# A 4-byte tile of ones is allocated behind the buffer of exponentials in a fused attention and MLP kernel

## The chip, the cores and the metric

One core of a Trainium2 chip runs the whole kernel. The metric is the device time of one execution in microseconds (us); the figure for a kernel is the median of its runs.

## The reference

Sliding-window attention over 8 batches, 8 heads, 576 positions and 64 features, then an MLP over the 4608 tokens of 512 features.

```python
scores = scale * np.matmul(q, k.transpose(0, 1, 3, 2))
mask = (rel >= 0) & (rel < window)                 # window = 128
scores = np.where(mask, scores + bias[None], -1000000000.0)
scores = scores - np.max(scores, axis=-1, keepdims=True)
attn = np.exp(scores)
attn = attn / (np.sum(attn, axis=-1, keepdims=True) + 1e-09)
attn_out = np.matmul(attn, v)
x = np.ascontiguousarray(attn_out.transpose(0, 2, 1, 3)).reshape(B * S, H * D)
h = x @ w_in                                       # 512 -> 2048
g = 0.5 * h * (1.0 + erf(h * inv_sqrt2))
return g @ w_out                                   # 2048 -> 512
```

## The kernel before

The tokens are cut into nine tiles of 512 (`t` = 0 to 8), and the attention into eight batches of four pairs of heads, 32 units. Batch 0 is computed in float32; from batch 1 on every operand is split into a high and a low float16 part, and a product is three matmuls. The order of all instructions is written out by hand in the table `ORDER`, so a change of addresses doesn't move any of them.

The attention of one batch after the first goes like this. `load_qk` brings q and k by DMA into two rooms, `ld_0` and `ld_1`, and `load_v` brings v into `v32`. `split_qk` and `split_v` write the two parts of each into `qbuf`, `kbuf` and `vbuf` (ScalarE the high part, VectorE at L335 the low one). `scores` multiplies them (L667), `biased` adds scale and bias into the tile `s` (L693), and `softmax` finds the maxima (L781) and the exponentials (L785) and scales them (L795). The high parts go into the buffer of exponentials `e_main` at L797 (L792 in batch 1) and `low_weights` puts the low parts there at L805 (L335 in batch 1). There is one `e_main`, [128 partitions, 9 groups, 2 parts, 256] in float16, for all units.

At L809 a DMA transpose, issued on SP's queue, then brings `e_main` into the tile `et`, in two pieces for each unit, one of five groups and one of four:

```python
yield nc.sync.dma_start_transpose(
    st.et[:, r.start * 4 : r.stop * 4, :], e[:, r].rearrange("p g h k -> p (g h k)")
)
```

Units with an even number write the buffer `et0`, those with an odd number `et1`. There are 28 such units, so 56 transposes. `weigh` multiplies `et` by `vbuf` on TensorE (L854), and `leave` writes the result into the tokens' tile `x`, which has two buffers used in turn.

The MLP multiplies `x` by `w_in` (L904 in the first three tiles, L1133 later, where sums of the tokens, `xs`, and of the weights, `t` from the DRAM tile `stored`, take part), applies GELU into `g`, and multiplies by `w_out` (L947, L950, and L1283 in the last two tiles). In the last two tiles `qbuf`, `kbuf`, `vbuf` and `e_main` are free and hold sums of weights that DMAs bring there (L1048, L1052). The sums are written to DRAM at L1041 from the rooms `ld_0` and `ld_1`, in turn.

The tile of ones, `one`, is a single float32 on one partition. It is set once (L288) and is the stationary operand of the 16 matmuls at L300, which spread a maximum over the partitions (`over_partitions` with `early`).

All of these tiles lie in one pool. A tile takes a multiple of 32 bytes of each partition, and tiles stand in memory in the order in which they are first asked for in the program's text.

Of the kernel before, what the change touches and what calls it, by code (L numbers as in the profile page):

```python
# [11 lines left out]
F32 = mybir.dt.float32  # L12
# [194 lines left out]
def attention_gelu_mlp(  # L207
# [10 lines left out]
    nc = tc.nc  # L218
    pool = ctx.enter_context(tc.tile_pool(name="sb", bufs=1))
# [64 lines left out]
    QP = 32  # L284
    square = pool.tile([QP, QP], F32, name="square")
    nc.vector.memset(square, 0.0)
    one = pool.tile([1, 1], F32, name="one")
    nc.vector.memset(one, 1.0)  # L288

    spreads = []  # L290

# [414 lines left out]
        yield nc.gpsimd.memset(e[:, ODD, :, 0:QB], 0.0)  # L706

    e_main = pool.tile([P, NG, 2, 256], F16, name="e_main")


    e_first = [e.rearrange(p).bitcast(F32)[:, 0 : NG * 256].rearrange("p (g k) -> p g k", g=NG)
# [805 lines left out]
```

## Time and profile before

| | |
|---|---|
| median of 3 runs | 874.44 us (871.98 to 876.07) |
| the profiled execution | 873.86 us, its span 872.1 us |
| granted TensorE clock | 0.998 |
| busy share of the span | PE 97%, DVE 81%, ACT 70%, POOL 39% |
| instructions | 19752 |

PE is TensorE's matmuls, PEld its weight loads, DVE VectorE, ACT ScalarE, POOL GpSimd and SP the engine that issues the DMAs. A matmul's busy time is modelled: matmuls overlap in the array, so a busy PE isn't always a PE at its peak. Idle time of an engine is shown beside what ended it. DMA transfers run on 16 DMA engines; a view of DMAs gives their busy share in tenths and the GB/s that they moved in 40 equal slices of the stretch that was asked for.

### The profile page before, as it was taken

What the parts mean: (1) busy time and instruction counts of PE and PEld (TensorE: products, weight loads), DVE (VectorE), ACT (ScalarE), POOL (GpSimd) and SP (SyncE); (2) the same over time, 40 slices, a digit from 0 to 9 for tenths busy, and PEclk for the clock granted to TensorE, in tenths of its full rate; (3) what the DMA queues carried; (4) which work ended last, traced back from release to release, by engine and by line L of the source; (5) the groups of instructions that cost most, each with busy time, mean ns of one, the idle gap of its engine ahead of it and who ended that gap; (6) DMA issues with size and microseconds to landing.
All of it is one profiled execution on the core that took longest, in us unless ns stands there. A gap on an engine that the chain in (4) does not pass through costs nothing.

```text
span 872.1 us, 19752 instructions
## 1 busy us (share of the span) xinstructions
PE 842.9 (97%) x7876; PEld 549.3 (63%) x7876; DVE 706.8 (81%) x1275; ACT 612.0 (70%) x1234; POOL 342.9 (39%) x553
## 2 busy tenths in 40 slices
PE   7899999999999999999999998998999999999997
PEld 4644444544544455884578556864587467888886
DVE  5998999899889966889797988799778656784772
ACT  6978879888769967775677776764776547753671
POOL 5731000033024774479635965576435670000000
PEclk9999999999999999999999999999999999999999
DMA  9855666642563557555846396447752493412301
GB/s 306 286 161 201 230 188 116 152 161 57 102 144 98 137 133 207 194 128 150 188 143 187 104 212 177 127 86 188 187 188 56 110 200 152 188 50 85 110 1 50
DMA packets 180940, 129.47 MB, mean 148 GB/s; under 512 B 134384, under 2 KB 157040, under 8 KB 177136
## 3 DMA queue, kind: packets, MB, share of 16 engines
q1 hardware_dynamic: 180848, 128.21, 53.3%
q8 instruction: 62, 1.02, 0.5%
q14 instruction: 30, 0.25, 0.1%
HBM read 75.89 MB, written 17.83 MB: 107 GB/s over the span
## 4 chain that ended last, share of the span: by engine, by line
PE 55%; DVE 19%; DMA 10%; ACT 8%; issue 4%; POOL 3%; SPq 0%; DVEq 0%; ACTq 0%; POOLq 0%
PE u L1133 12%; PE v L1133 9%; PE h L904 9%; DMA et<-e_main 7%; PE o L950 6%; PE o L947 5%; PE u_out L1283 4%; DMA k<-kp 3%; DVE g L335 3%; PE sc L667 3%; DVE s L693 2%; DVE e_main L805 2%; DVE nmax L781 2%; PE av L854 1%; PE z_out L1283 1%
## 5 line engine op out<-in xcount | busy, mean ns | idle before, releaser
L950 PEld LDWEIGHTS <-g 128*128 128x128 f16 x1152 | 111.0, 98 | 131.2
L950 PE MATMUL o<-wo,g 128*128 128x512 f16 x864 | 192.2, 379 | 0.0
L785 ACT ACTIVATE s<-s,nmax 128x192 f32<-128x192 f32 x252 | 112.0, 446 | 46.8 <-DVE nmax L781 46.5
L904 PE MATMUL h<-x,wi 128*128 128x512 f16 x576 | 128.6, 379 | 1.9 <-DVE wi L335 1.6
L795 POOL TENSOR_SCALAR s<-s,z 128x192 f32<-128x192 f32 x180 | 100.9, 576 | 25.0 <-DVE z L789 11.5
L1133 PEld LDWEIGHTS <-t 128*128 128x128 f16 x1008 | 98.4, 98 | 11.8
L904 PEld LDWEIGHTS <-wi 128*128 128x128 f16 x576 | 54.8, 98 | 67.8 <-DVE wi L335 1.9
L1133 PEld LDWEIGHTS <-wi 128*128 128x128 f16 x864 | 83.9, 98 | 13.4 <-issue 1.3
L699 POOL MEMSET s<- 64x128 f32 (+1 forms) x112 | 19.3, 173 | 157.2 <-DVE s L693 143.6
L693 DVE SCALAR_TENSOR_TENSOR s<-sc,cs,bias_h 128x384 f32<-128x384 f32 x112 | 65.6, 606 | 2.0 <-PE sc L667 1.1
L950 PE MATMUL o<-wo_moved,g 128*128 128x512 f16 x288 | 66.0, 379 | 0.0
L781 DVE TENSOR_REDUCE nmax<-s 128x5 f32<-128x960 f32 (+1 forms) x56 | 58.4, 1047 | 3.4 <-POOL s L699 2.5
L1133 PE MATMUL u<-xs,t 128*128 128x256 f16 x504 | 59.9, 273 | 0.0
L947 PE MATMUL o<-zo,g 128*128 128x512 f32 x128 | 57.6, 599 | 0.0
L854 PE MATMUL av<-et,vbuf 128*64 128x128 f16 (+2 forms) x1392 | 43.7, 220 | 13.7 <-DMA et<-e_main 13.7
L805 DVE TENSOR_TENSOR e_main<-s,e_main 128x960 f16<-128x960 f32 (+1 forms) x40 | 46.5, 1168 | 11.4 <-ACT e_main L797 11.3
L667 PE MATMUL sc<-kbuf,qbuf 64*64 64x192 f16 (+3 forms) x1656 | 49.3, 251 | 6.3 <-DMA kbuf<-kp 4.6
L854 PEld LDWEIGHTS <-vbuf 128*64 128x64 f16 x1392 | 40.3, 111 | 23.4 <-issue 17.9
L1184 POOL TENSOR_SCALAR g<-rooms,sg 128x512 f16<-128x512 f32 x48 | 39.5, 830 | 24.7 <-ACT rooms L1178 21.5
L785 ACT ACTIVATION_READ_ACCUMULATOR s<-s,nmax 128x1 f32 x252 | 47.7, 189 | 0.0
L335 DVE SCALAR_TENSOR_TENSOR g<-rooms,sg,g 128x512 f16<-128x512 f32 x48 | 40.6, 864 | 8.0 <-POOL g L1184 7.9
L797 ACT CAST e_main<-s 128x960 f16<-128x960 f32 (+1 forms) x40 | 36.1, 907 | 14.5 <-POOL s L795 10.4
(256 smaller groups left out, 1698.6 us busy)
## 6 DMA issues: line engine op xcount, KB each, us to landing
t<-stored SPq DMA_DIRECT2D x21, 1024.0 KB, 5.2
v<-vp SPq DMA_DIRECT2D x32, 320.0 KB, 5.4
out<-ob SPq DMA_DIRECT2D x34, 256.0 KB, 2.8
raw<-w_in SPq DMA_DIRECT2D x8, 1024.0 KB, 10.7
raw<-w_out SPq DMA_DIRECT2D x8, 1024.0 KB, 6.1
q<-qp SPq DMA_DIRECT2D x7, 1152.0 KB, 5.8
k<-kp SPq DMA_DIRECT2D x7, 1152.0 KB, 7.1
stored<-sums SPq DMA_DIRECT2D x8, 512.0 KB, 2.7
```

The source lines that it names most:

```text
L335: return nc.vector.scalar_tensor_tensor(out=dst, in0=src, scalar=scale, in1=high, op0=ALU.mult, op1=ALU.subtract)
L667: done = nc.tensor.matmul(ps[bank][o, n, gap:W], a, m[:, gap:W], start=(i == 0 and (n == 0 or b > 0)), stop=(i == len(terms) - 1 and b > 0 ...
L693: yield nc.vector.scalar_tensor_tensor(out=s[:, bank[0] : bank[0] + k, :], in0=ps[bank][:, 0:k, 0:W], scalar=cs, in1=bias.broadcast_to([P, ...
L781: yield nc.vector.tensor_reduce(out=nmax[:, r], in_=s[:, r], axis=AX.X, op=ALU.max, negate=True)
L785: yield nc.scalar.activation(s[:, i, :], s[:, i, :], AF.Exp, bias=nmax[:, i : i + 1], accum_out=z[:, i : i + 1])
L795: yield nc.gpsimd.tensor_scalar(to, s[:, i], z[:, i : i + 1], 1.0, op0=ALU.mult, op1=ALU.mult)
L805: yield engine.tensor_tensor(out=e[:, r, 1, c], in0=st.s[:, r], in1=e[:, r, 0, c], op=ALU.subtract)
L854: done = nc.tensor.matmul(av[r, (js[0] - blocks[0]) * QB : (js[-1] + 1 - blocks[0]) * QB], v32s[b][:, hp, kb, r] if b < EXACT else vbuf[:, ...
L904: done = nc.tensor.matmul(ph, wi[n][:, a, cc, k * P : (k + 1) * P], x[:, cc, b, :], start=(i == 0), stop=(i == 3 * NCC - 1),)
L947: done = nc.tensor.matmul(o, g[:, r, c], zo[n][:, n % 2, k * DM : (k + 1) * DM], start=(fc == first), stop=(fc == last))
L950: done = nc.tensor.matmul(o, g[:, r, a, c], (wo if t else wo_first)[n][:, b, k, :], start=(fc == first and i == 0), stop=(fc == last and i ...
L1133: done = nc.tensor.matmul(ps[:, k * HT : (k + 1) * HT], w(a, i)[:, k * P : (k + 1) * P], m(b, i), start=first and n == 0, stop=True, skip_ ...
```

## The change

The two lines that allocate `one` and set it to 1 move from behind the tile `square` to behind `e_main`.

```diff
     square = pool.tile([QP, QP], F32, name="square")
     nc.vector.memset(square, 0.0)
-    one = pool.tile([1, 1], F32, name="one")
-    nc.vector.memset(one, 1.0)
...
     e_main = pool.tile([P, NG, 2, 256], F16, name="e_main")
+    one = pool.tile([1, 1], F32, name="one")
+    nc.vector.memset(one, 1.0)
```

On VectorE, at the start of the program, the memset of `one` stands here before (`adders` holds the identity matrices):

```order
L260 MEMSET adders 128x128
L286 MEMSET square 32x32
L288 MEMSET one 1x1
L264 COPY adders<-adders 64x64 x4
L265 COPY adders<-adders 128x64
```

and here in the changed program:

```order
L260 MEMSET adders 128x128
L286 MEMSET square 32x32
L708 MEMSET one 1x1
L264 COPY adders<-adders 64x64 x4
L265 COPY adders<-adders 128x64
```

It has kept its place, and so has every other instruction on every engine and queue, with its waits. What differs is where tiles lie. Byte at which a tile starts in each partition, in the two built programs:

```
tile                        bytes   before    after   after minus before
square                        128     6272     6272     0
one                            32     6400    45056     +38656
pww, sww, ... s2 (8 tiles)     32 each, 6432 to 6656 before    -32
qbuf                         9216     6688     6656     -32   (before 13*512 + 32)
kbuf                         9728    15904    15872     -32   (before 31*512 + 32)
vbuf                        10240    25632    25600     -32   (before 50*512 + 32)
e_main                       9216    35872    35840     -32   (before 70*512 + 32)
x, one of its two buffers    8192    45088    45088     0     (32 past a multiple of 64)
x, the other                 8192   129920   129920     0     (a multiple of 64)
et0                          9216    75552    75552     0     (32 past a multiple of 64)
et1                          9216   112448   112448     0     (a multiple of 64)
ld_0                         9216    84768    84768     0     (32 past a multiple of 64)
ld_1                         9216   175040   175040     0     (a multiple of 64)
g, two of four               8192    60320, 121696      0     (32 past a multiple of 64)
g, the other two             8192   104256, 138112      0     (multiples of 64)
```

All other tiles stay where they were. In the table a multiple of 64 is never one of 256, but for the four large buffers that move, which start at multiples of 512 after the change.

## Rows read from the trace of the kernel before

**Rows 1.** The page, parts 1 and 2: busy time of the engines; busy tenths by slice.
```profile
PE 842.9 (97%) x7876; PEld 549.3 (63%) x7876; DVE 706.8 (81%) x1275; ACT 612.0 (70%) x1234; POOL 342.9 (39%) x553
...
PE   7899999999999999999999998998999999999997
...
PEclk9999999999999999999999999999999999999999
```

**Rows 2.** The list of waits: who waited for whom, us in total, times, longest.
```profile
PE av L854 <- DMA et<-e_main: 13.7, 10, 2.9
...
PEld L854 <- DMA et<-e_main: 5.5, 3, 2.1
...
PE sc L667 <- DMA kbuf<-kp: 4.6, 1, 4.6
```

**Rows 3.** The view of line 854: idle time of its engine (us, times) until
```profile
  DMA et<-e_main: 19.2, 13
```

**Rows 4.** The chain that ended last: shares by line; pieces (start us, us).
```profile
PE u L1133 12%; PE v L1133 9%; PE h L904 9%; DMA et<-e_main 7%; PE o L950 6%; PE o L947 5%; PE u_out L1283 4%; DMA k<-kp 3%; DVE g L335 3%; PE sc L667 3%; DVE s L693 2%; DVE e_main L805 2%; DVE nmax L781 2%; PE av L854 1%; PE z_out L1283 1%
...
149.12 5.41 DMA et<-e_main
...
709.31 6.61 DMA et<-e_main
```

**Rows 5.** The tile e_main: duration in ns (min/median/max), first and last start; landings.
```profile
L809 SPq DMA_TRANSPOSE et<-e_main x56: 1541/3066/5885, 119.2 to 713.0; - x56
L797 ACT CAST e_main<-s x40: 816/906/994, 275.8 to 710.8; 128x960 f16<-128x960 f32 x20, 128x768 f16<-128x768 f32 x20
L805 DVE TENSOR_TENSOR e_main<-s,e_main x40: 943/1147/1701, 278.9 to 711.6; 128x960 f16<-128x960 f32 x20, 128x768 f16<-128x768 f32 x20
...
DMA to landing us min/median/max: 4.2/5.0/9.8
```

**Rows 6.** DMAs of the stretch 206 to 213 us (slices of 0.175 us).
```profile
GB/s 0 0 0 0 0 0 0 0 0 0 10 170 221 218 203 209 217 215 227 214 217 221 214 219 222 215 215 168 119 87 224 214 217 206 209 217 218 224 214 218
DMA packets 4105, 1.04 MB, mean 149 GB/s; under 512 B 4105, under 2 KB 4105, under 8 KB 4105
```

**Rows 7.** DMAs of the stretch 220 to 229.5 us (slices of 0.24 us).
```profile
GB/s 0 0 0 0 0 0 0 0 87 224 213 204 221 217 218 217 218 216 213 212 182 103 205 212 168 27 8 188 292 287 290 291 285 6 0 0 0 0 0 0
DMA packets 4673, 1.19 MB, mean 125 GB/s; under 512 B 4672, under 2 KB 4672, under 8 KB 4672
```

**Rows 8.** DMA issues of the stretch 257 to 261 us (KB each, us to landing).
```profile
stored<-sums SPq DMA_DIRECT2D x1, 512.0 KB, 2.8
```

**Rows 9.** DMAs of the stretch 266 to 271 us (slices of 0.125 us).
```profile
GB/s 12 0 0 0 0 0 0 0 0 0 0 0 0 0 0 0 0 197 328 426 426 426 360 426 426 393 459 328 0 0 0 0 0 0 0 0 0 0 0 0
...
stored<-sums SPq DMA_DIRECT2D x1, 512.0 KB, 2.6
```

**Rows 10.** Views of the tiles x, e_main and g, and of line 1133: duration in ns.
```profile
L904 PE MATMUL h<-x,wi x576: 376/379/390, 35.5 to 298.3; 128*128 128x512 f16 x192
...
L1133 PE MATMUL u<-xs,t x504: 269/273/283, 359.5 to 837.4; 128*128 128x256 f16 x168
...
L1283 PE MATMUL u_out<-e_main,slots x48: 272/273/273, 787.0 to 862.2; 128*128 128x256 f16 x48
...
L1283 PE MATMUL u_out<-wo,g x72: 272/273/283, 737.2 to 846.5; 128*128 128x256 f16 x72
...
L1224 ACT ACTIVATE g<-room_s,sg x24: 708/723/727, 726.0 to 856.6; 128x512 f16<-128x512 f32 x24
L335 DVE SCALAR_TENSOR_TENSOR g<-room_s,sg,g x24: 741/749/754, 726.7 to 857.4; 128x512 f16<-128x512 f32 x24
```

**Rows 11.** The tile one: duration in ns (min/median/max).
```profile
L300 PEld LDWEIGHTS spread<-red,one x16: 180/182/184, 28.4 to 124.3; 1*128 1x128 f32 x16
...
L288 DVE MEMSET one<- x1: 59/59/59, 1.0 to 1.0; 1x1 f32 x1
```

## The prediction, made before the changed kernel ran

> **What bounds the kernel now.** Start with the page's busy times [rows 1]. TensorE is busy 842.9 of 872.1 us, at nine tenths or more in nearly every slice, at the full granted clock. So an edit that leaves its matmuls alone can win only what TensorE idles, 872.1 - 842.9 = 29.2 us, and an edit that delays something off TensorE costs only what comes through to it. Then read the list of waits for the idle time that has an address in it [rows 2]. The largest such item is the wait of the matmuls and weight loads of L854 for the transposed exponentials: 13.7 + 5.5 = 19.2 us, 13 times, which the view of that line confirms [rows 3]. The chain that ended last passes through the same transposes [rows 4]: 7% of it lies in ten pieces between 149 and 716 us, of which the first and the last are shown. The share says where the path runs; it doesn't say how much of it would be saved, for where a transpose lands sooner TensorE takes up the slack after 19.2 us at most.
>
> **What the change removes, adds and moves.** It adds no instruction and takes none away, and on no queue does one pass another. The memset of 59 ns [rows 11] keeps its place on VectorE, and the 16 weight loads of `one`, 180 to 184 ns each, read the same single number from another address. I cost both at zero; there is no cover to lose, because nothing has moved in time. What is left is the 32 bytes by which `qbuf`, `kbuf`, `vbuf` and `e_main` slide down: from 32 past a multiple of 512 to a multiple of 512. So the sum has one kind of term, the price of an address. I take it apart by who uses these buffers.
>
> *TensorE, ScalarE, VectorE.* The trace already holds both kinds of address for them. The 576 matmuls at L904 read the two buffers of `x` in turn, one at a multiple of 64 and one 32 past it, and all take 376 to 390 ns. L1133 reads `xs`, 32 past a multiple of 64, in 273 ns; L1283 reads `e_main`, 32 past, in 273 ns, and `wo` in the same 273. ScalarE writes four buffers `g`, two of each kind, in 708 to 727 ns, and VectorE in 741 to 754 [rows 10]. The spread over both kinds is under 3%, so the term is zero, with ends that I can't tell from zero.
>
> *The first loads and the last.* The four loads each of q and k at the start land in buffers that move, and TensorE waits 4.6 us for one [rows 2]. The end of the gain is some part of that once; I take zero. The six loads of weight sums at the end appear in no wait of TensorE in the list, so their price is hidden by the matmuls of the stretch.
>
> *The 56 transposes.* This is the term that matters. Each reads `e_main` and lands after 4.2 to 9.8 us, median 5.0 [rows 5]. The larger piece moves 128 partitions x 5 groups x 512 numbers x 2 bytes = 655 KB, and its packets are all under 512 bytes [rows 6]. Its steady rate is about 217 GB/s, so 655 KB take 3.02 us of the landing. Is that rate set by an address? For the destination the trace answers: those of the one stretch write `et0`, 32 past a multiple of 64 [rows 6], those of the other stretch `et1`, at a multiple [rows 7], and both run at 203 to 227 GB/s, mostly 213 to 221. For the source no transpose of the trace has another address, since there is one `e_main`. The nearest row is another DMA that reads the same memory: the store of sums at L1041 lands after 2.8 us from `ld_0`, 32 past a multiple of 64 [rows 8], and after 2.6 us from `ld_1`, a multiple [rows 9]. The 0.2 us between them lies within what a slice of these rows can tell, and neither start is a multiple of 256. I take **zero for each transpose**, and keep both ends for the range. The end of the gain: packets of 4 KB leave at about 426 GB/s [rows 9], by which 655 KB would take 1.54 us, 1.48 less; and the transposes themselves reach 285 to 292 GB/s in one burst [rows 7], by which it would be 2.26 us, 0.76 less. So a faster rate exists, and what holds the rest at 217 isn't shown. The end of the loss: the slowest landing is 9.8 us where the median is 5.0, but that one is a transfer among others and no price of an address; nothing in the rows makes a source at a round address slower, so I take only VectorE's spread for it (the slower rival).
>
> *Sum.* The profiled execution took 873.86 us, span 872.1 and 1.76 us around it. 873.86 + 0 = 873.9 us. That stands 0.6 us under the median of the three runs, 874.44, and well within their spread of 4 us. A measurement of this kernel can tell about 0.5%, 4.4 us, from no change.
>
> **The rivals.** *The transposes' rate rises.* If each transpose of the larger size went at the burst's 290 GB/s, it would land 0.76 us sooner. TensorE waits 13 times [rows 3], so 13 x 0.76 = 9.9 us, under the 19.2 us that there are: 873.9 - 9.9 = 864 us. For it: a higher rate is in the trace, and every packet is small, so a fixed cost of a packet weighs much. Against it: destinations of both kinds give one rate, and a store from either kind gives nearly one time. It passes 4.4 us from 0.34 us a transpose on, a rate of 655 / 2.68 = 245 GB/s. The Trainium skill, in "DMA: Bandwidth & Descriptors", section "Latency and other measured facts", gives a transposing DMA 261 GB/s with a non-contiguous layout and more with a contiguous one; the 217 here are below both, and by 261 the larger piece would take an estimated 2.51 us, 0.51 less.
>
> *A packet loses the part that lies across a boundary.* A row of 128 numbers is 256 bytes. Before, each starts 32 bytes past a multiple of 256 and ends 32 bytes in the next stretch of 256; after, it lies in one. As a mechanism of this kernel: nine pieces of 32 bytes, one of them unused, would be eight. That takes one ninth off the 3.02 us, 0.34 us, and with 13 waits 4.4 us: 869.5 us, right at the bound. If the fixed cost of a packet doesn't shrink along, it is less: the burst at 290 GB/s has the same packets at 2.26 us, one ninth of which is 0.25 us, 13 x 0.25 = 3.3 and 870.6 us. The Trainium skill, in "DMA: Bandwidth & Descriptors", section "How a descriptor splits into AXI transactions", states such a split: a descriptor that begins past a 256-byte boundary is read from the boundary below it, in one transaction more. No row here shows it, since no DMA between two tiles of this memory with one start at a multiple of 256 stands beside one without; the two stores can't [rows 8, 9], as both start off one.
>
> *Slower: the writes into e_main get in each other's way.* VectorE's subtraction at L805 takes 943 to 1701 ns for two shapes, median 1147 [rows 5], so something already stretches some of them. If the round address made all of them as slow as the slowest, 0.55 us each over the median, the transposes behind them would leave later, and at the 13 places where TensorE waits for `et` it would wait on: 13 x 0.55 = 7.2 us, 881 us. It decides from 0.34 us on, a median of 1.49 us at L805. Against it: ScalarE's cast into the same buffer is steady at 816 to 994 ns for its two shapes, and neither engine shows a price of an address [rows 10].
>
> *The change does nothing at all*, because the buffers were rounded to some boundary anyway: excluded by the addresses of the built programs but for a fault in them; it gives 873.9 us too.
>
> **How the numbers follow.** No price of an address that reaches TensorE: 0.52. The boundary's part: 0.18, half of it over 4.4 us and half under. The higher rate: 0.18. Writes in each other's way: 0.10. Nothing done: 0.02. So faster by over 0.5%: 0.18 + 0.09 = 0.27; within it: 0.52 + 0.09 + 0.02 = 0.63; slower: 0.10. The forecast is that of the likeliest case, 873.9 us. The range goes down to 866, a gain of 0.6 us at each of 13 waits, which takes in the boundary's part and the smaller third of the higher rate, and up to 878, 4 us of runs or a little of the slower rival; about 0.13 is left out below and 0.06 above.
>
> **What would show it.** Right: in the changed profile the transposes still go at about 217 GB/s, their landing stays near 5.0 us, TensorE still idles some 19 us before L854, and no group's duration moves by over 3%. A median landing under 4.7 us, or a steady rate over 245 GB/s, with less idle time before L854, shows the first or the second rival; 4.8 with a rate near 230 is the boundary's part alone. A median over 1.4 us at L805 shows the slower one. The prediction is wrong if the time is off by more than 4.4 us, and wrong in its reason if the transposes change their rate and the time doesn't follow.

## The result and the profile after

The changed kernel takes 864.56 us in the median of 4 runs (862.44 to 865.7), the kernel before 874.0 in the median of 4 (871.98 to 876.07). The ratio is 0.9889, with a 95% interval of 0.9857 to 0.9921: 1.1% faster, where no difference was forecast, and 1.4 us under the lower end of the range. The profiled execution took 865.7 us, its span 863.9, 8.2 us less than the 872.1 before.

The page of the changed kernel, busy time of TensorE and the chain that ended last by line:

```profile
PE 843.2 (98%) x7876; PEld 549.7 (64%) x7876; DVE 707.0 (82%) x1275; ACT 609.7 (71%) x1234; POOL 341.0 (39%) x553
...
PE h L904 13%; PE u L1133 13%; PE o L950 11%; PE v L1133 9%; PE o L947 7%; PE u_out L1283 4%; DMA k<-kp 3%; DMA et<-e_main 3%; PE av L854 3%; PE sc L665 2%; DVE g L333 1%; DVE e_main L805 1%; PE z_out L1283 1%; PE x_out L1283 1%; PE y_out L1283 1%
```

TensorE is busy as long as it was, 843.2 against 842.9 us [rows 1]. What shrank is its idle time: 863.9 - 843.2 = 20.7 us, from 29.2. The transposes' part of the chain fell from 7% to 3% [rows 4]. The view of line 854 says how long its engine waited for them (us, times), in the changed kernel:

```profile
  DMA et<-e_main: 9.0, 7
```

Before it was 19.2 us, 13 times [rows 3]. This view adds up two rows of TensorE that run side by side, the matmuls (PE) and the weight loads (PEld). The list of waits keeps them apart; in the changed kernel (us, times, longest):

```profile
PE av L854 <- DMA et<-e_main: 6.1, 5, 2.3
...
PEld L854 <- DMA et<-e_main: 2.8, 2, 1.8
```

The three waits of PEld in the kernel before [rows 2] are no places of their own: each ends at the same time as one of the ten waits of PE. The timeline of the kernel before shows it for one of them (start and duration in us, idle time before it in brackets):

```profile
249.11 0.20 PEld L854 LDWEIGHTS <-vbuf 128*64 128x64 f16 x6 [1.66 <-DMA et<-e_main]
249.11 0.30 PE L854 MATMUL av<-et,vbuf 128*64 128x128 f16 x4 [1.45 <-DMA et<-e_main]
```

So the matmuls waited for `et` 13.7 us at ten places before, and 6.1 us at five after. Of the 8.5 us that TensorE idles less, this wait gave some 7.6. Another 1.5 lies behind the last matmul, where the span runs on for 5.0 us before and 3.5 after; it is 3.5 as well in the run below that has `e_main` alone off, so this part isn't the address's. Other waits took about 0.5 back.

A wait may cost more than its length. In the profiled execution of the changed kernel TensorE's matmuls sat idle until 527.23 us, for 2.25 us, waiting for `et`. Right behind that the granted clock (the third number from the end) stood at its lower level, 0.50 or 1.2 GHz:

```profile
527.40:530.60 3.20, 3.20 (x62) 2.70 (x59) 3.01 (x4) 1.69 (x4) 3.20 (x1) 0.50 0.44 113
```

In the kernel before it stayed at 1.00 behind the same wait, of 2.95 us. How much of the gain is clock wasn't measured.

The tile `e_main` shows why the wait is shorter (duration in ns, min/median/max; us to landing):

```profile
L797 ACT CAST e_main<-s x40: 814/904/993, 272.6 to 705.8; 128x960 f16<-128x960 f32 x20, 128x768 f16<-128x768 f32 x20
L805 DVE TENSOR_TENSOR e_main<-s,e_main x40: 943/1146/1682, 275.7 to 706.7; 128x960 f16<-128x960 f32 x20, 128x768 f16<-128x768 f32 x20
...
L1283 PE MATMUL u_out<-e_main,slots x48: 272/272/273, 780.4 to 855.6; 128*128 128x256 f16 x48
...
DMA to landing us min/median/max: 3.6/4.2/10.0
```

ScalarE, VectorE and TensorE take for `e_main` what they took before, 904 against 906 ns, 1146 against 1147, 272 against 273 in the medians [rows 5, 10]. Only the transposes differ: a median of 4.2 us to landing instead of 5.0. The view of DMAs, stretch 202 to 211 us of the changed kernel, slices of 0.225 us, holds the same two transposes as [rows 6]:

```profile
GB/s 0 0 0 0 0 0 0 0 0 0 0 0 0 0 0 0 0 0 69 282 289 291 289 291 291 289 291 288 225 24 198 289 290 289 291 291 289 289 97 0
DMA packets 4672, 1.18 MB, mean 131 GB/s; under 512 B 4672, under 2 KB 4672, under 8 KB 4672
```

The steady rate is 290 GB/s where it was 217, with packets as small as before. For 655 KB that is 2.26 us instead of 3.02, 0.76 us less.

### The profile page after: what moved, and what is told of

It is laid out like the page before. It is cut to its first block, busy times and chain, and to the rows that moved or that the text cites. A ratio compares the mean times of both kernels' runs of the same rounds, so it can differ in the third digit from the quotient of the medians.

```text
span 863.9 us, 19752 instructions
## 1 busy us (share of the span) xinstructions
PE 843.2 (98%) x7876; PEld 549.7 (64%) x7876; DVE 707.0 (82%) x1275; ACT 609.7 (71%) x1234; POOL 341.0 (39%) x553
## 4 chain that ended last, share of the span: by engine, by line
PE 67%; DVE 12%; DMA 9%; ACT 4%; issue 4%; POOL 3%; SPq 1%; POOLq 0%; DVEq 0%; ACTq 0%
PE h L904 13%; PE u L1133 13%; PE o L950 11%; PE v L1133 9%; PE o L947 7%; PE u_out L1283 4%; DMA k<-kp 3%; DMA et<-e_main 3%; PE av L854 3%; PE sc L665 2%; DVE g L333 1%; DVE e_main L805 1%; PE z_out L1283 1%; PE x_out L1283 1%; PE y_out L1283 1%
## 5 line engine op out<-in xcount | busy, mean ns | idle before, releaser
L904 PE MATMUL h<-x,wi 128*128 128x512 f16 x576 | 128.6, 379 | 1.7 <-DVE wi L333 1.4
L904 PEld LDWEIGHTS <-wi 128*128 128x128 f16 x576 | 54.8, 98 | 67.6 <-issue 2.0
L1133 PEld LDWEIGHTS <-wi 128*128 128x128 f16 x864 | 84.0, 98 | 13.7 <-issue 1.7
L697 POOL MEMSET s<- 64x128 f32 (+1 forms) x112 | 19.2, 172 | 156.0 <-DVE s L691 137.8
L805 DVE TENSOR_TENSOR e_main<-s,e_main 128x960 f16<-128x960 f32 (+1 forms) x40 | 45.7, 1149 | 13.1 <-ACT e_main L797 13.0
L854 PEld LDWEIGHTS <-vbuf 128*64 128x64 f16 x1392 | 41.0, 113 | 15.3 <-issue 12.4
L854 PE MATMUL av<-et,vbuf 128*64 128x128 f16 (+2 forms) x1392 | 44.2, 223 | 6.1 <-DMA et<-e_main 6.1
```

What stands on the lines that cost most here:

```text
L805: yield engine.tensor_tensor(out=e[:, r, 1, c], in0=st.s[:, r], in1=e[:, r, 0, c], op=ALU.subtract)
L854: done = nc.tensor.matmul(av[r, (js[0] - blocks[0]) * QB : (js[-1] + 1 - blocks[0]) * QB], v32s[b][:, hp, kb, r] if b < EXACT else vbuf[:, ...
L904: done = nc.tensor.matmul(ph, wi[n][:, a, cc, k * P : (k + 1) * P], x[:, cc, b, :], start=(i == 0), stop=(i == 3 * NCC - 1),)
L1133: done = nc.tensor.matmul(ps[:, k * HT : (k + 1) * HT], w(a, i)[:, k * P : (k + 1) * P], m(b, i), start=first and n == 0, stop=True, skip_ ...
```

## The experiments

Each full kernel below has the instructions of the changed kernel in the same order; only tiles lie elsewhere. The ratios are to the kernel before as it ran beside them: 872.76 us in the median for the first two, 873.01 for the other full kernels.

**Which buffer: e_main alone off.** `one` is allocated just ahead of `e_main`, which pushes `e_main` alone back to 32 past a multiple of 512.

```diff
-    e_main = pool.tile([P, NG, 2, 256], F16, name="e_main")
     one = pool.tile([1, 1], F32, name="one")
     nc.vector.memset(one, 1.0)
+    e_main = pool.tile([P, NG, 2, 256], F16, name="e_main")
```

> The changed kernel with e_main alone back at 32 past a multiple of 512, qbuf, kbuf and vbuf at multiples of 512. Theory, e_main's address in the transposes is the whole effect: the time of the kernel before, 874 us (871 to 877), transposes at 217 GB/s, TensorE idle for et some 19 us. Rival, the address of qbuf, kbuf and vbuf carries it: 864.6 us. Rival, both have a part: in between, 867 to 871.

Measured: 873.06 us, ratio to the kernel before 1.0004 (0.9989 to 1.0018). The whole gain is gone.

**Which buffer: e_main alone on.** `e_main` and `one` are allocated ahead of `qbuf`, so that `e_main` starts at 13*512 and `qbuf`, `kbuf` and `vbuf` at 32 past a multiple of 512, as in the kernel before.

```diff
+    e_main = pool.tile([P, NG, 2, 256], F16, name="e_main")
+    one = pool.tile([1, 1], F32, name="one")
+    nc.vector.memset(one, 1.0)
     qbuf = pool.tile([P, 2, NPAIR * S], F16, name="qbuf")
...
-    e_main = pool.tile([P, NG, 2, 256], F16, name="e_main")
-    one = pool.tile([1, 1], F32, name="one")
-    nc.vector.memset(one, 1.0)
```

> The changed kernel with e_main at a multiple of 512, but qbuf, kbuf and vbuf at 32 past one, as in the kernel before. Theory, e_main alone: 864.6 us (862 to 867), transposes at 290 GB/s. Rival, the other three carry it: 874 us. Both have a part: 867 to 871.

Measured: 863.83 us, ratio 0.9903 (0.987 to 0.9937). The whole gain is there without the other three buffers. The transposes land after 5.0 us in the median with `e_main` alone off and after 4.2 with it alone on. The wait of L854 for the transposes, first with `e_main` alone off, then with `e_main` alone on (PE and PEld added up, as above):

```profile
  DMA et<-e_main: 14.8, 11
```

```profile
  DMA et<-e_main: 6.4, 7
```

With `e_main` alone off the wait is under the expected some 19 us, but the time came as expected: TensorE is busy 845.3 us there, against 842.9 in the kernel before, and that isn't traced to a cause. The two runs bracket the effect from both sides: the address of `e_main` is it, and the other addresses that the change moves are worth nothing that can be measured.

**Which price, and from which multiple on: the transposes by themselves.** This kernel leaves out the whole computation and issues transposes of 655 KB back to back, then plain copies in pieces of 256 bytes.

`dst` holds three tiles.

```diff
+SRC = (0, 32, 64, 96, 128, 192, 224, 256, 288, 480)
+DST = (0, 32, 64, 128, 160)
+COLS = 2560
...
+        for d in DST:
+            for s in SRC if d == 0 else (0, 32):
+                for t in dst:
+                    nc.sync.dma_start_transpose(
+                        t[:, d // 2 : d // 2 + COLS].rearrange("p (n k) -> p n k", k=P), src[:, s // 2 : s // 2 + COLS]
+                    )
```

> Nothing of the reference is computed; the kernel only issues DMAs between tiles of the on-chip memory and writes zeros out. Groups of three transposes of 655 KB follow each other: sources at 0, 32, 64, 96, 128, 192, 224, 256, 288 and 480 bytes past a multiple of 512 with the destination at 0; then destinations at 32, 64, 128 and 160 with sources at 0 and 32; at the end plain copies in pieces of 256 bytes with sources at 0, 32, 64, 128 and 256. Theory, a read of 256 bytes that crosses a multiple of 256 costs more: about 290 GB/s for sources at 0 and 256, about 217 for all others (3.0 against 2.26 us a transpose), the destination makes no difference. Rival, multiples of 64 matter: 290 also at 64, 128 and 192. Rival, multiples of 512 matter: 290 at 0 alone. Rival, the address isn't the cause: one rate for all.

The view by stretches (us, busy times, clock, share of the DMA engines, GB/s in the last column). Each stretch lies inside one setting; which one follows from the order and the equal number of packets. First the destination at a multiple of 512 and the source 0, 32, 64, 128, 256 and 288 past one:

```profile
5.50:12.50 7.00, 0.00 (x0) 0.00 (x0) 1.00 1.14 259
14.00:22.00 8.00, 0.00 (x0) 0.00 (x0) 1.00 1.12 211
24.00:31.50 7.50, 0.00 (x0) 0.00 (x0) 1.00 1.10 207
43.00:50.50 7.50, 0.00 (x0) 0.00 (x0) 1.00 1.12 210
71.00:77.50 6.50, 0.00 (x0) 0.00 (x0) 1.00 1.10 251
79.00:87.00 8.00, 0.00 (x0) 0.00 (x0) 1.00 1.10 208
```

Then destination and source 32 and 0, 32 and 32, 128 and 0, 160 and 0 past a multiple of 512:

```profile
98.00:105.00 7.00, 0.00 (x0) 0.00 (x0) 1.00 1.11 252
107.00:115.00 8.00, 0.00 (x0) 0.00 (x0) 1.00 1.10 206
133.50:140.50 7.00, 0.00 (x0) 0.00 (x0) 1.00 1.11 252
151.00:158.50 7.50, 0.00 (x0) 0.00 (x0) 1.00 1.11 252
```

Sources at 0 and 256 go at 251 to 259 GB/s, the others shown at 206 to 211, wherever the destination is; the stretches of 96, 192, 224 and 480 lie at 206 to 211 too. It is multiples of 256 of the source that count, neither of 64 nor of 512. These means lie under the 290 and 217 of the kernels because they take in the dips between one transpose and the next. The view of DMAs of 5 to 14 us, slices of 0.225 us, shows three transposes from source 0 and then, from about 13 us on, the start of the first from 32 past:

```profile
GB/s 64 276 290 289 291 289 290 289 291 291 239 13 155 290 288 290 291 289 290 290 291 290 148 9 204 291 288 291 291 291 290 288 291 280 98 18 185 217 210 199
```

Inside a transpose the rates are the kernels' own. The plain copies at the end agree, with 288 GB/s from source 0, 294 from 256, 215 from 64 and 216 from 128. Only the stretch of the source 32 past has 244, because its first part still goes at 290; the last section comes back to this.

**The same in the kernel: 192 past a multiple of 256.** Two small tiles move behind `e_main`, so that the four buffers start at a multiple of 64 that is none of 256.

```diff
-    pww = pool.tile([P, NWP], F32, name="pww")
-    sww = pool.tile([P, NWP], F32, name="sww")
...
     e_main = pool.tile([P, NG, 2, 256], F16, name="e_main")
     one = pool.tile([1, 1], F32, name="one")
     nc.vector.memset(one, 1.0)
+    pww = pool.tile([P, NWP], F32, name="pww")
+    sww = pool.tile([P, NWP], F32, name="sww")
```

> The changed kernel with two small tiles (pww, sww) moved behind e_main, so that qbuf, kbuf, vbuf and e_main all start at 448 past a multiple of 512: a multiple of 64, but 192 past one of 256. Theory, a 256-byte read across a multiple of 256: every read crosses, transposes back at about 217 GB/s, time of the kernel before, 873 us (871 to 876), TensorE idle for et 15 to 19 us. Rival, multiples of 64 (or 32 and 64) are what counts: 864 us and 290 GB/s.

Measured: 872.61 us, ratio 0.9999 (0.998 to 1.0018), and L854 waits for the transposes as follows. The time is the kernel before's, and the idle time lies a little under the expected 15 to 19.

```profile
  DMA et<-e_main: 13.3, 10
```

**The same in the kernel: a multiple of 256, not of 512.** All eight small tiles (`pww` to `s2`) move behind `e_main` in the same way.

> The changed kernel with eight small tiles moved behind e_main, so that qbuf, kbuf, vbuf and e_main start at 256 past a multiple of 512. Theory, 256: no read crosses, 864 us (862 to 867), transposes at about 290 GB/s, TensorE idle for et 6 to 9 us. Rival, multiples of 512: 873 us and 217 GB/s.

Measured: 862.97 us, ratio 0.9893 (0.9867 to 0.9919). The tile `e_main` and line 854 of this run:

```profile
DMA to landing us min/median/max: 3.7/4.2/10.0
```

```profile
  DMA et<-e_main: 5.5, 6
```

Both as the theory says: the boundary is 256.

**Is there more in the destinations?** `et0` and `et1` are allocated behind `e_main`, at 88*512 and 106*512.

```diff
     e_main = pool.tile([P, NG, 2, 256], F16, name="e_main")
+    for n in range(2):
+        pool.tile([P, NG * 4, P], F16, tag=f"et{n}", name=f"et{n}_room", bufs=1)
     one = pool.tile([1, 1], F32, name="one")
```

> The changed kernel with the two destinations of the transposes, et0 and et1, at multiples of 512 too (they stand at 288 and 320 past one before). Theory, only the source counts: 864 us, no change that can be told from the changed kernel, landing of the transposes 4.2 us as there. Rival, a write across a boundary costs as well: the rate rises above 290 GB/s, the landing falls under 4 us, and the time to 860 us or less, which would beat both kernels.

Measured: 864.06 us, ratio to the kernel before 0.9903 (0.9873 to 0.9933), with a landing of 4.1 us in the median. That can't be told from the changed kernel. The four versions with `e_main` on the boundary lie at 862.97 to 864.56 us, closer together than the runs of any one of them spread.

**Why the stores of sums showed nothing.** Plain copies of 1024 KB, six for each setting, with nothing else in the kernel but a write of zeros.

```diff
+SRC = (0, 32, 192, 256)
+PIECES = (256, 512, 1024, 4096)
...
+        for size in PIECES:
+            k = size // 2
+            for s in SRC:
+                for t in dst * 2:
+                    nc.sync.dma_start(
+                        t.rearrange("p (n k) -> p n k", k=2 * k)[:, :, 0:k],
+                        src[:, s // 2 : s // 2 + 4096].rearrange("p (n k) -> p n k", k=k),
+                    )
```

> Nothing of the reference is computed; the kernel only copies between tiles of the on-chip memory with plain DMAs and writes zeros out. Six copies of 1024 KB each for every pair of a piece (256, 512, 1024, 4096 bytes) and a source that starts 0, 32, 192 or 256 bytes past a multiple of 512. Theory, a piece that doesn't start at a multiple of 256 costs one more stretch of 256, some 4 ns on a DMA engine, whatever its length: pieces of 256 lose about a fifth of their rate at 32 and 192 against 0 and 256, of 512 a tenth, of 1024 about a twentieth, and of 4096 about a hundredth, which explains why the stores of sums with their large pieces showed nothing. Rival, only transposes pay: all four sources give one rate at every length. Rival, large pieces pay as much in proportion: a fifth at 4096 too.

The view by stretches, GB/s in the last column. Pieces of 256 bytes with sources 0, 32, 192 and 256 past a multiple of 512, then of 512, of 1024 and of 4096 bytes in the same order:

```profile
10.00:25.00 15.00, 0.00 (x0) 0.00 (x0) 1.00 1.28 290
32.00:54.00 22.00, 0.00 (x0) 0.00 (x0) 1.00 0.85 216
60.00:83.00 23.00, 0.00 (x0) 0.00 (x0) 1.00 1.04 216
89.00:105.00 16.00, 0.00 (x0) 0.00 (x0) 1.00 1.28 290
110.00:123.00 13.00, 0.00 (x0) 0.00 (x0) 1.00 1.15 348
128.00:144.00 16.00, 0.00 (x0) 0.00 (x0) 1.00 1.02 307
149.00:165.00 16.00, 0.00 (x0) 0.00 (x0) 1.00 1.05 285
171.00:184.00 13.00, 0.00 (x0) 0.00 (x0) 1.00 1.15 347
189.00:200.00 11.00, 0.00 (x0) 0.00 (x0) 1.00 1.09 386
205.00:217.00 12.00, 0.00 (x0) 0.00 (x0) 1.00 1.09 386
222.00:235.00 13.00, 0.00 (x0) 0.00 (x0) 1.00 1.04 340
240.00:252.00 12.00, 0.00 (x0) 0.00 (x0) 1.00 1.09 386
256.00:266.00 10.00, 0.00 (x0) 0.00 (x0) 1.00 1.02 419
271.00:281.00 10.00, 0.00 (x0) 0.00 (x0) 1.00 1.03 421
286.00:296.00 10.00, 0.00 (x0) 0.00 (x0) 1.00 1.02 421
301.00:312.00 11.00, 0.00 (x0) 0.00 (x0) 1.00 1.03 421
```

Pieces of 256 bytes go at 290 or 216 GB/s, almost to the number the two rates of the transposes in the kernels: the price belongs to the read of a small piece, not to the transposing. With longer pieces it fades, and at 4096 bytes there is none. The theory of a fixed price for each piece holds in part. On one of the 16 engines a piece of 256 bytes takes 16 x 256 / 290 = 14.1 ns or 19.0 ns, 4.9 more; one of 512 takes 3.1 (32 past) or 5.2 ns more (192 past), one of 1024 nothing (32 past) or 5.7 (192 past), and one of 4096 nothing, where the theory still had a hundredth. Why the distance matters for the longer pieces is open. These copies stay in the on-chip memory, while the stores of sums go to DRAM; no run stored to DRAM from a source on the boundary.

## Why the prediction was wrong

*What bounds the kernel* held: TensorE's busy time didn't change, and most of what the profiled executions differ by, 7.6 of 8.2 us, came out of the waits for `et`. But these were 13.7 us at ten places, not 19.2 at 13: the sum 13.7 + 5.5 counts three of them twice.

*The terms at zero* held for the memset of `one` (59 ns in the same place), for TensorE, ScalarE and VectorE, and for the loads at the start and the end: with `e_main` alone on, the other three buffers at their old offset cost nothing that shows. One reading was loose: the 376 to 390 ns of L904 spread by 3.7%, not under 3%.

*The step that failed* is "zero for each transpose", where 0.76 of 3.02 us was measured, and in it the choice of the nearest row. The stores of sums from `ld_0` and `ld_1` read the same memory, but in large pieces [rows 8, 9]; the copies of 4096 bytes show 419 to 421 GB/s for sources on and off a multiple of 256, so, if a store to DRAM reads as these copies do, such rows couldn't have shown the price, wherever the rooms stood. The row that was nearest in the thing that counted, the size of a piece, was the transposes' own burst at 285 to 292 GB/s [rows 7], which stood in the prediction as an end of the range. The text also saw that both stores start off a multiple of 256, and still gave the case that rests on them 0.52.

*The rival of the higher rate* gave the outcome: 0.76 us a transpose, 13 waits, 864 us. Measured are 290 GB/s, 0.76 us, and 864.56. That the sum agrees so closely is luck in part. With the ten places it is 10 x 0.76 = 7.6 us, as much as the matmuls' wait fell by in the profiled executions; the rest of the 9.4 us between the medians isn't traced to a cause. Its chance was 0.18.

*The rival of the boundary* had the right cause and too small a price. It took one ninth off a transpose, 0.34 us or with the burst's rate 0.25; a quarter of it went, 0.76 of 3.02 us. The Trainium skill's "DMA: Bandwidth & Descriptors", section "How a descriptor splits into AXI transactions", puts the boundary at 256 bytes, and the runs agree: sources at 0 and 256 are fast, at 64, 128 and 192 slow. By its count a piece that starts 32 past would cost 9 beats of 32 bytes instead of 8, an estimated 12% more time, and one that starts 192 past 14, an estimated 75% more; measured is 19.0 ns at both against 14.1, 35% more, so the measurement decides. In a steady flow a piece of 256 bytes pays here for crossing the boundary, and equally wherever it crosses. The Trainium skill's 261 GB/s for a transposing DMA with a non-contiguous layout, on the same page in the section "Latency and other measured facts", lies between the two rates measured here, 217 and 290.

*The slower rival* fell: the subtraction at L805 has a median of 1146 ns against 1147, and the longest is 1682 against 1701.

*The bounds* were too narrow below. With a rival at 864 us and a chance of 0.18, the range ended at 866 because two thirds of that rival were left out.

## What to carry to other kernels

Where a DMA reads the on-chip memory in pieces of 256 bytes, as a transposing one does, put the buffer it reads at a multiple of 256 bytes: here that raised its rate from 217 to 290 GB/s, and a small tile in front of it was enough to lose that. The place of the destination didn't matter to a transpose, nor that of the source to pieces of 4096 bytes; pieces of 512 and 1024 paid less. When a price is bounded by the nearest row, that row must be near in the quantity by which the price would scale, here the size of a piece, and not only in where it reads. And where a view adds up rows that run side by side, its count of waits isn't a count of places.

## What was not expected of the hardware

In the kernel before, one burst at the end of a transpose runs at 285 to 292 GB/s although its source is off the boundary [rows 7], and the kernel with the source 192 past a multiple of 256 shows the like in its stretch from 217 to 229 us:

```profile
GB/s 0 0 0 0 0 0 0 0 0 0 0 0 0 0 0 0 79 224 212 212 218 218 218 218 216 211 132 176 211 109 9 145 289 289 291 281 3 0 0 0
```

These aren't the only ones. The kernel before has such a burst at twelve places at least, as here between 408 and 414 us (slices of 0.15 us; the first slices and the last hold other transfers too):

```profile
GB/s 430 445 353 338 314 301 353 236 111 36 3 0 2 9 9 10 9 10 184 287 292 292 290 290 292 283 295 287 292 292 441 355 423 437 178 55 382 410 437 437
```

Each of the twelve follows a gap of 0.4 to 1.5 us at almost nothing, which begins some 500 packets into a transpose. A gap between two transposes doesn't do it: in the run of transposes alone, the one at 13 us falls to 18 GB/s, and what follows from 32 past goes at 185 to 217. The plain copies of 256 bytes show something alike. The six from source 0 hold 6.29 MB, but the rate stays at 289 GB/s from 6.7 to 30.5 us, for 6.9 MB, so the first 0.6 MB from 32 past also went at the full rate.

So a read off the boundary doesn't pay every time. That packets pass at the full rate after a stop within a transfer would fit reads that were made ahead during it; no run here tested that.
